# A recurrence and a dense layer in one kernel: sharing weight pieces between two leading units, loading operands once, and filler products

## The chip, the cores and the metric

The kernel runs on one core of one Trainium2 chip. The metric is device time in microseconds (us); a median of several executions is given with lowest and highest. The trace of one execution has its own length, the span, which is a few us shorter (before: 714.8 us span, 716.6 us as that execution was timed). Before the change the time is 720.13 us, median of 3 runs (718.22 to 721.48). No run below is marked as slow in the record, so all can be compared, and all gave the right result.

Engines: TensorE (PE in the profile; PEld is its loading of stationary operands), VectorE (DVE), ScalarE (ACT), GpSimd (POOL), SyncE (SP). PEclk is the clock granted to TensorE, as a share of full speed.

## The reference

```python
batch, n_heads, seq, head_dim = 4, 8, 768, 48        # d_model = 384, d_ff = 2048
for t in range(S):                                    # gated recurrence, per head
    state = alpha[:, :, t, :, None] * state + einsum('bhd,bhe->bhde', k[:, :, t], v[:, :, t])
    y[:, :, t] = einsum('bhd,bhde->bhe', q[:, :, t], state)
x = y.transpose(0, 2, 1, 3).reshape(B * S, H * D)     # 3072 tokens x 384
h = x @ w_in                                          # dense part
out = (h - tanh(h)) @ w_out
```

The weights arrive as 8-byte floats; the kernel converts them on the chip.

## The kernel before

Work is cut into 12 units of 256 tokens, three per batch. Each unit has a recurrence (`gla`), done in two chunks of 128 tokens, and a dense part (`moe`) of eight pieces: for each piece 12 matmul records (entries of the trace; a product of the program shows as two) of a first product `h`, a shrink (four instructions on ScalarE, three on VectorE), and 8 records of a second product `o`. While the dense part of one unit runs, the recurrence of the next is threaded between its pieces. The order on every engine is fixed by positions in a list:

```python
put(at, do, *args)        # one step of work at position `at`; all are sorted by `at` and issued in that order
...
moe(0, (31, 34, 37, 46, 53, 60, 68, 76), (40, 43, 50, 57, 65, 72, 79.5, 83))
STEP = 6.6
for u in range(1, NU):
    t0 = 78 + (u - 1) * FS * STEP                     # unit u's pieces follow those of unit u-1
    moe(u, [t0 + s * STEP for s in range(FS)], [t0 + (s + 2.5) * STEP for s in range(FS)])
```

At the start the weights are converted piece by piece (16 pieces): two ScalarE instructions, three VectorE instructions (source lines L65, L67, L69), one GpSimd addition. Unit 0 uses each piece as it becomes ready; unit 1 begins when unit 0 is done.

One chunk of the recurrence on TensorE, with what reads its results:

```python
def back():      tp = ps_y.tile(..., name="tp", tag="tp")       # 4 transposes of kT
def natural():   A.copy(kn, tp)                                 # ScalarE
def update():    up = ps_y.tile(..., name="up", tag="tp")       # up = kn * v, in the bank of tp
def state():     V.tensor_add(new, old, up)                     # VectorE, the state sum
def scores():    sc0, sc1 = ps_sc.tile(...), ps_sc.tile(...)    # k * q, a bank for each half of the heads
def masked():    V.tensor_mul(pm, sc, mask)
def products():  y = ps_y.tile(..., name="y", tag="y")          # from pm, v and the old state
```

TensorE's results go to PSUM. The Trainium skill, "PSUM — Partial Sum Buffer", Specifications (TRN2), gives eight banks of 512 FP32 values per partition. The program agrees: two for `h`, two for `sc0` and `sc1`, one for `y`, one that `tp` and `up` share, two for the accumulators `o0` and `o1`. All eight are taken.

## Time and profile before

| | before |
|---|---|
| time | 720.13 us (718.22 to 721.48) |
| span, granted clock | 714.8 us, 0.975 |
| TensorE / VectorE / ScalarE busy | 87% / 63% / 46% |
| first product `h` of unit 0, of unit 2 | 44.7 us, 183.0 us (the prediction has 183.1) |
| TensorE from unit 2's first product to its last | 524.2 us |

The prediction shows the slices and the waits of the first 160 us. For the rest, these are all of TensorE's waits after 180 us (columns: engine, operation, source line, what it waited for; then us in total, times, longest):

```profile
PE up L503 <- ACT kn L497: 12.5, 9, 1.6
PE sc L451 <- POOL qT L417: 9.6, 9, 1.4
PE tp L492 <- POOL kT L417: 1.7, 2, 0.8
```

So 23.8 us of 535 are lost in the steady part, nearly all of it at two places of each unit: before `up` and before `sc`.

### The profile page before, as it was taken

The page shows a single profiled execution, that of the slowest core. Times are in us where ns is not written, and L with a number is a line of the kernel's source. Part 1 is how long each engine was busy: PE and PEld are TensorE (multiplying, and loading weights), DVE is VectorE, ACT ScalarE, POOL GpSimd, SP SyncE. Part 2 cuts the span into 40 slices and gives each one's busy share as a digit, 9 for nine tenths or more (in the row PEclk, how much of TensorE's full clock was granted, in tenths as well). Part 3 has the DMA queues.
Part 4 walks back from the last instruction along what each step waited for, and adds up shares of the span by engine and source line. Part 5 has one row for each costly group of instructions (what it writes and reads, how often), then busy time and mean ns, then how long its engine had stood idle before and what let it go on. Part 6 is the DMA issues. An engine that isn't in the chain of part 4 may idle for free.

```text
span 714.8 us, 8728 instructions
## 1 busy us (share of the span) xinstructions
PE 621.6 (87%) x3089; PEld 460.4 (64%) x3089; DVE 451.3 (63%) x639; ACT 329.2 (46%) x701; POOL 115.9 (16%) x98
## 2 busy tenths in 40 slices
PE   0655586879989989989989989989989989989995
PEld 0543365657757767767767667767767767767773
DVE  4749877783683783682783773773874864874341
ACT  1435355544544544544634534634544444444451
POOL 2522543130020030030020120030110120120000
PEclk9978799999999999999999999999999999999998
DMA  9996556300801701701702602602603503500000
GB/s 181 213 178 146 107 141 164 58 1 18 160 1 28 150 1 31 146 1 37 141 1 55 122 1 54 124 1 60 118 1 81 97 1 81 98 0 7 23 0 28
DMA packets 57268, 50.99 MB, mean 71 GB/s; under 512 B 29440, under 2 KB 52096, under 8 KB 57216
## 3 DMA queue, kind: packets, MB, share of 16 engines
q1 hardware_dynamic: 54560, 49.20, 33.0%
q10 hardware_dynamic: 2656, 1.15, 1.0%
q8 instruction: 26, 0.43, 0.3%
q14 instruction: 26, 0.21, 0.1%
HBM read 44.43 MB, written 4.72 MB: 69 GB/s over the span
## 4 chain that ended last, share of the span: by engine, by line
PE 45%; DVE 27%; DMA 15%; POOL 5%; issue 3%; ACT 2%; SPq 2%; DVEq 0%; POOLq 0%; ACTq 0%
PE h L534 21%; PE o L558 15%; DVE W L411 6%; DMA qr<-in_q_dram 6%; DMA raw<-in_moe_w_in_dram 4%; DMA ar<-in_alpha_dram 3%; PE sc L451 3%; DVE kT L381 3%; DVE qT L381 3%; DVE z L546 3%; POOL qT L417 3%; DVE U L395 3%; PE y L476 3%; DVE w L545 3%; DVE aT L381 3%
## 5 line engine op out<-in xcount | busy, mean ns | idle before, releaser
L534 PE MATMUL h<-xT,w_in 128*128 128x256 f32 x1152 | 275.8, 391 | 22.9 <-POOL w_in L72 15.3
L558 PE MATMUL o<-w_out,g 128*128 128x384 f32 x768 | 267.0, 491 | 11.4 <-POOL w_out L72 11.4
L534 PEld LDWEIGHTS h<-xT,w_in 128*128 128x128 f32 x1152 | 221.7, 195 | 72.1 <-POOL w_in L72 17.6
L558 PEld LDWEIGHTS o<-w_out,g 128*128 128x128 f32 x768 | 144.3, 191 | 95.3 <-POOL w_out L72 13.1
L542 ACT ACTIVATE u<-h 128x512 f32<-128x512 f32 x96 | 57.3, 597 | 244.2 <-PE h L534 244.2
L545 DVE TENSOR_TENSOR w<-h,u 128x512 f32<-128x512 f32 x96 | 65.6, 683 | 162.6 <-ACT u L542 162.4
L417 POOL TENSOR_TENSOR kT<-kT,U 128x1024 f32<-128x1024 f32 (+1 forms) x13 | 30.3, 2331 | 377.1 <-DVE least L404 377.1
L546 DVE SCALAR_TENSOR_TENSOR z<-z,w 128x512 f32<-128x512 f32 x96 | 83.5, 869 | 10.6 <-DVE w L545 0.9
L547 DVE SCALAR_TENSOR_TENSOR g<-z,z 128x512 f32<-128x512 f32 x96 | 67.3, 701 | 10.4 <-ACT big L549 0.5
L543 ACT ACTIVATE z<-u 128x512 f32<-128x512 f32 x96 | 60.5, 630 | 3.1
L549 ACT ACTIVATE big<-u 128x512 f32<-128x512 f32 x96 | 58.9, 614 | 0.0
L544 ACT ACTIVATE z<-u 128x512 f32<-128x512 f32 x96 | 58.9, 613 | 0.0
L411 DVE TENSOR_TENSOR_SCAN W<-aT,before 128x1032 f32<-128x1032 f32 x12 | 48.7, 4059 | 0.4
L458 DVE TENSOR_TENSOR pm<-sc,mask 128x512 f32<-128x512 f32 x46 | 29.6, 685 | 16.9 <-PE sc L451 16.5
L503 PE MATMUL up<-vt,kn 128*128 128x96 f32 x160 | 22.8, 287 | 18.8 <-ACT kn L497 18.8
L417 POOL TENSOR_TENSOR qT<-qT,W 128x1024 f32<-128x1024 f32 (+1 forms) x13 | 26.7, 2053 | 65.6 <-DVE qT L381 65.6
L451 PE MATMUL sc<-qT,kT 48*128 48x128 f32 x368 | 27.6, 291 | 10.5 <-POOL qT L417 10.5
L451 PEld LDWEIGHTS sc<-qT,kT 48*128 48x128 f32 x368 | 23.1, 193 | 20.8 <-POOL qT L417 16.7
L503 PEld LDWEIGHTS up<-vt,kn 128*128 128x128 f32 x160 | 20.8, 198 | 22.6 <-ACT kn L497 22.0
L483 ACT COPY xs<-y 48x128 f32<-48x128 f32 x48 | 12.5, 260 | 46.5 <-PE y L476 46.2
L512 DVE TENSOR_TENSOR state<-state,up 48x192 f32<-48x192 f32 x32 | 11.2, 350 | 34.7 <-PE up L503 33.4
L492 PE MATMUL tp<-ident,kT 128*128 128x128 f32 x80 | 13.2, 291 | 20.1 <-POOL kT L417 20.1
(60 smaller groups left out, 444.0 us busy)
## 6 DMA issues: line engine op xcount, KB each, us to landing
raw<-in_moe_w_out_dram SPq DMA_DIRECT2D x8, 768.0 KB, 4.6
ar<-in_alpha_dram SPq DMA_DIRECT2D x24, 192.0 KB, 3.7
qr<-in_q_dram SPq DMA_DIRECT2D x24, 192.0 KB, 6.9
raw<-in_moe_w_in_dram SPq DMA_DIRECT2D x16, 288.0 KB, 7.8
out_dram<-ob SPq DMA_DIRECT2D x24, 192.0 KB, 1.9
ar<-in_alpha_dram SPq DMA_DIRECT2D x24, 176.0 KB, 4.1
qr<-in_q_dram SPq DMA_DIRECT2D x24, 176.0 KB, 6.9
kr<-in_k_dram SPq DMA_DIRECT2D x22, 192.0 KB, 5.3
```

What stands on the lines that cost most here:

```text
L381: V.transpose(t[:, g].rearrange("p c (i r) -> p r c i", r=R), raw[:, g, :, 0:32])
L411: V.tensor_tensor_scan(out=W.rearrange("p n t -> p (n t)"), data0=aT[:, 0:N * (P + 1)], data1=before, initial=0.0, op0=ALU.mult, op1=ALU.add)
L417: GP.tensor_mul(t, t, m[by].rearrange("p (g c) t -> p g c t", c=CU)[:, :, cs, 1:])
L451: T.matmul(sc[hh][:, g, :], lhsT=m["kT"][q, g, c, :], rhs=m["qT"][q, g, c, :], start=True, stop=True)
L534: T.matmul(h[:, a, :], lhsT=w_in[:, j, f * P:(f + 1) * P], rhs=xT[u][:, j, :], start=(j == 0), stop=(j == KT - 1))
L543: A.activation(z1, sq, AF.Square, bias=QB1, scale=QA)
L544: A.activation(z2, sq, AF.Square, bias=QB2, scale=QA)
L545: V.tensor_mul(w, h, sq)
L546: V.scalar_tensor_tensor(out=z1, in0=z1, scalar=QK1, in1=w, op0=ALU.add, op1=ALU.mult)
L547: V.scalar_tensor_tensor(out=g, in0=z2, scalar=QK2, in1=z1, op0=ALU.add, op1=ALU.mult)
L549: A.activation(big, sq, AF.Relu, bias=-U_MAX, accum_out=over[:, n:n + 1])
L558: T.matmul(o[c], lhsT=g[:, a * TU + c * P:a * TU + (c + 1) * P], rhs=w_out[:, f, :], start=(f == 0), stop=(f == FT - 1))
```

## The change

Its intent: the start is slow because pieces of weights trickle in and one unit does not have enough work for each. Let units 0 and 1 both use a piece as it comes. That needs four output accumulators, hence two more PSUM banks, which `y` and `tp`/`up` give up. To free the DMA queues, each operand is loaded once, and the shifted second copy is made on the chip (`widen`, six ScalarE copies per unit). Fillers keep TensorE's clock up in three waits of the first 36 us. Cut to its core:

```diff
-        ps_y = ctx.enter_context(tc.tile_pool(name="ps_y", bufs=1, space=PSUM))
...
-                    for dq in range(2):                       # load: each operand twice, shifted by 32
-                        queue.dma_start(out=t[at:at + 32]..., in_=src[:, :, 32 * dq:])
+                queue.dma_start(out=t[HP * hh:HP * hh + 32]..., in_=...)          # once
...
+            def aside(name):                                  # bank of y, and of tp and up
+                if u < 2:
+                    return ps_o.tile(..., tag="o2" if name == "y" else "o3")
+                return ps_sc.tile(..., tag="sc0" if name == "y" else "sc1")
+            def widen(what, hh):
+                to, of = t[r0 + 32:r0 + HP, :, :, 0:D - 32], t[r0:r0 + 32, :, :, 32:D]
+                A.copy(to, of)                                # one of unit 0 on VectorE
...
-                    y = m["y"] = ps_y.tile(..., name="y", tag="y")
+                    y = m["y"] = aside("y")                   # likewise tp and up
...
-                o.extend(ps_o.tile([P, d_model], FP32, name=f"o{c}") for c in range(CU))
+                o.extend(ps_o.tile([P, d_model], FP32, name=f"o{CU * (u % 2) + c}") for c in range(CU))
...
+        put(1, spin, 36); put(17, spin, 8); put(28.5, spin, 22)        # identity times identity
...
-        moe(0, (31, 34, 37, 46, 53, 60, 68, 76), (40, 43, 50, 57, 65, 72, 79.5, 83))
+        moe(0, (34, 37, 43, 50, 57, 65, 76, 87), (40, 46, 53, 59, 68, 79, 90, 97))
+        moe(1, (62, 71, 82, 93, 98.5, 104, 109.5, 115), (74, 84.5, 95.5, 101, 106.5, 112, 117.5, 123))
...
-                           scores=(18, 27), ..., back=(13, 30), update=(15.5, 33), moves=36.5)
+                           scores=(19, 29), ..., back=(13, 23), update=(15, 25.5), moves=38)
```

More of the change, by code (lines that the diff above doesn't have):

```diff
@@ L298, in fast @@
         for t, x in zip(raws, (1.0, 0.0, 0.0)):
-            V.memset(t[:, :, R - 1, :], x)
+            for hh in range(2):
+                V.memset(t[HP * hh + 32:HP * hh + HP, :, :, D - 32:32], x)
         N = NP * CU
@@ L314, in fast @@
             GP.memset(t, 0.0)
+        wake = consts.tile([P, 1], FP32, name="wake")
+        V.memset(wake, 1.0)
+        A.activation(wake, wake, AF.Square)
         raw_in, raw_out = {}, {}
@@ L349, in fast, with load @@
         vts, xT = {}, {}
-        def load(u):
+        def load(u, what, queue):
             b, i = divmod(u, UPB)
             t0 = i * TU
-            other = A if u == 0 else nc.sync
-            for n, (t, x) in enumerate(zip(raws, (alpha, k, q))):
-                queue = other if n == 1 else nc.sync
-                for hh in range(2):
-                    src = x[b].rearrange("(g two) s d -> two g (s d)", two=2)[hh][:, t0 * D:(t0 + TU) * D]
-                    src = src.rearrange("g (i n) -> i g n", i=32)
-                    for dq in range(2):
-                        at = 64 * hh + 32 * dq
-                        queue.dma_start(
-                            out=t[at:at + 32].rearrange("p g r d -> p g (r d)")[:, :, 0:R * D - 32 * dq],
-                            in_=src[:, :, 32 * dq:])
-            vt = vts[u] = three.tile([P, CU, H, D], FP32, name="vt")
-            for c in range(CU):
-                other.dma_start(out=vt[:, c], in_=v[b, :, t0 + c * P:t0 + (c + 1) * P, :].rearrange("h p d -> p h d"))
+            if what == 3:
+                vt = vts[u] = three.tile([P, CU, H, D], FP32, name="vt")
+                for c in range(CU):
+                    queue.dma_start(out=vt[:, c],
+                                    in_=v[b, :, t0 + c * P:t0 + (c + 1) * P, :].rearrange("h p d -> p h d"))
+                return
+            t, x = raws[what], (alpha, k, q)[what]
+            for hh in range(2):
+                src = x[b].rearrange("(g two) s d -> two g (s d)", two=2)[hh][:, t0 * D:(t0 + TU) * D]
+                queue.dma_start(out=t[HP * hh:HP * hh + 32].rearrange("p g r d -> p g (r d)"),
+                                in_=src.rearrange("g (i n) -> i g n", i=32))
         def gla(u, at):
@@ L376, in gla @@
             m = {}
+            def aside(name):
+                if u < 2:
+                    return ps_o.tile([P, NP, P], FP32, name=name, tag="o2" if name == "y" else "o3")
+                return ps_sc.tile([P, NP, P], FP32, name=name, tag="sc0" if name == "y" else "sc1")
             def flip(raw, make):
@@ L385, in new @@
                 return m[name]
+            def widen(what, hh):
+                t, r0 = raws[what], HP * hh
+                to, of = t[r0 + 32:r0 + HP, :, :, 0:D - 32], t[r0:r0 + 32, :, :, 32:D]
+                if u == 0 and what == 0 and hh == 1:
+                    V.tensor_copy(to, of)
+                else:
+                    A.copy(to, of)
+            for what, name in enumerate(("aT", "kT", "qT")):
+                for hh in range(2):
+                    put(at[name] - 1.5, widen, what, hh)
             put(at["aT"], flip, raws[0], lambda: tail[:, :, 0:P].rearrange("p (g c) t -> p g c t", c=CU))
@@ L468, in products @@
                 def products():
-                    y = m["y"] = ps_y.tile([P, NP, P], FP32, name="y", tag="y")
+                    y = m["y"] = aside("y")
                     if n > 0:
@@ L489, in back @@
                 def back():
-                    tp = m["tp"] = ps_y.tile([P, NP, P], FP32, name="tp", tag="tp")
+                    tp = m["tp"] = aside("tp")
                     for g in range(NP):
@@ L500, in update @@
                 def update():
-                    up = m["up"] = ps_y.tile([P, NP, 2, D], FP32, name="up", tag="tp")
+                    up = m["up"] = aside("up")[:, :, 0:2 * D].rearrange("p g (two d) -> p g two d", d=D)
                     for g in range(NP):
@@ L522, in moves @@
                         r0 = HP * hh + f0 - (H - 2 + hh) * D
-                        nc.sync.dma_start(out=xT[u][part, j, :], in_=m["xs"][r0:r0 + part.stop - part.start])
+                        (A if u < 2 else nc.sync).dma_start(out=xT[u][part, j, :], in_=m["xs"][r0:r0 + part.stop - part.start])
             put(at["moves"], moves)
@@ L570, in moe, with spin @@
             put(second_at[-1] + 2.8, store)
-        put(0, load, 0)
-        for at, what, s in ((0.1, fetch_in, 0), (0.2, fetch_in, 1), (0.3, fetch_out, 0), (0.4, fetch_in, 2)):
-            put(at, what, s)
-        put(20, load, 1)
+        def spin(n):
+            t = ps_o.tile([P, P], FP32, name="spin", tag="o0")
+            for _ in range(n):
+                T.matmul(t, lhsT=ident, rhs=ident, start=True, stop=True)
+        put(0, load, 0, 0, nc.sync)
+        put(0, load, 0, 1, A)
+        put(0.1, load, 0, 2, nc.sync)
@@ L577, in fast @@
+        put(0.1, load, 0, 3, A)
+        put(0.2, fetch_in, 0)
+        put(9, load, 1, 0, nc.sync)
+        put(9.1, fetch_in, 1)
+        put(14, load, 1, 1, nc.sync)
+        put(14, load, 1, 3, nc.sync)
+        put(17, load, 1, 2, nc.sync)
+        put(17.1, fetch_out, 0)
+        put(17.2, fetch_in, 2)
         for s in range(1, FS):
-            put(31 + 6 * s, fetch_out, s)
+            put(17 + 6 * s, fetch_out, s)
             if s + 2 < FS:
-                put(34 + 6 * s, fetch_in, s + 2)
@@ L581, in fast @@
-        gla(0, dict(aT=6, U=8, kT=10.3, ends=12.3, kTU=12.4, W=12.8, qT=15.2, qTW=17.2, sizeU=13.5, sizeW=18,
-                    scores=(19.4, 21.4), masked=(21.4, 23.4), decay=(0, 19.5), y=(23.4, 25.4), x=(25.3, 28),
-                    back=(14.5, 24.9), update=(16.2, 27.6), moves=29))
-        gla(1, dict(aT=34.5, U=38, kT=41.5, ends=43.5, kTU=45, W=46, qT=49, qTW=52, sizeU=42, sizeW=50,
-                    scores=(55.5, 62), masked=(57, 64), decay=(56, 63), y=(59, 67), x=(62, 70),
-                    back=(47, 68), update=(56, 70), moves=74))
@@ L587, in fast @@
-        for s, at in enumerate((15, 24.4, 28.7, 41, 48.7, 56, 64, 71)):
+                put(18 + 6 * s, fetch_in, s + 2)
+        put(1, spin, 36)
+        put(17, spin, 8)
+        put(28.5, spin, 22)
+        gla(0, dict(aT=5, U=7.5, kT=9.8, ends=11.8, kTU=11.9, W=12.3, qT=14.7, qTW=16.7, sizeU=10, sizeW=17,
+                    scores=(19, 21), masked=(21, 23), decay=(0, 19), y=(23, 25), x=(25, 27.5),
+                    back=(14, 24.5), update=(16, 27), moves=28))
+        gla(1, dict(aT=24, U=26, kT=28.5, ends=32.5, kTU=32.6, W=33, qT=37, qTW=39.5, sizeU=30, sizeW=38,
+                    scores=(43.5, 49.5), masked=(45.5, 51.5), decay=(40, 47), y=(48.5, 54), x=(51, 56.5),
+                    back=(37.5, 44.5), update=(39.5, 47), moves=57))
@@ L588, in fast @@
+        for s, at in enumerate((15, 20.5, 39, 45, 52, 62, 73, 84)):
             convert(at, round_in, s)
-        for s, at in enumerate((26.6, 37.5, 45, 52.5, 60, 67.5, 75, 79)):
+        for s, at in enumerate((29.5, 42, 48, 55, 65, 76, 87, 93)):
             convert(at, round_out, s)
-        moe(0, (31, 34, 37, 46, 53, 60, 68, 76), (40, 43, 50, 57, 65, 72, 79.5, 83))
+        moe(0, (34, 37, 43, 50, 57, 65, 76, 87), (40, 46, 53, 59, 68, 79, 90, 97))
+        moe(1, (62, 71, 82, 93, 98.5, 104, 109.5, 115), (74, 84.5, 95.5, 101, 106.5, 112, 117.5, 123))
@@ L593, in fast @@
         STEP = 6.6
-        for u in range(1, NU):
-            t0 = 78 + (u - 1) * FS * STEP
+        for u in range(2, NU):
+            t0 = 118 + (u - 2) * FS * STEP
             moe(u, [t0 + s * STEP for s in range(FS)], [t0 + (s + 2.5) * STEP for s in range(FS)])
-            if u > 1:
-                r = t0 - 46
-                put(r - 8, load, u)
-                rel = dict(aT=0, U=2.5, kT=5.5, ends=8, kTU=8, W=8.5, qT=11.5, qTW=14, sizeU=9, sizeW=12,
-                           scores=(18, 27), masked=(20, 29), decay=(16, 27), y=(23.5, 32), x=(26, 35),
-                           back=(13, 30), update=(15.5, 33), moves=36.5)
-                gla(u, {n: (r + x if not isinstance(x, tuple) else tuple(r + y for y in x))
-                        for n, x in rel.items()})
+            r = t0 - 46 if u > 2 else 75
+            for what in range(4):
+                put(r - 8 if u > 2 else 50, load, u, what, nc.sync)
+            rel = dict(aT=0, U=2.5, kT=5.5, ends=8, kTU=8, W=8.5, qT=11.5, qTW=14, sizeU=9, sizeW=12,
+                       scores=(19, 29), masked=(21, 31), decay=(16, 26.5), y=(24.5, 34), x=(27, 37),
+                       back=(13, 23), update=(15, 25.5), moves=38)
+            gla(u, {n: (r + x if not isinstance(x, tuple) else tuple(r + y for y in x))
+                    for n, x in rel.items()})
@@ L617, in fast @@
         V.tensor_reduce(out=fine[:, 0:1], in_=fine, axis=AX.X, op=ALU.min)
-        row = ps_y.tile([P, P], FP32, name="row", tag="tp")
+        row = ps_sc.tile([P, P], FP32, name="row", tag="sc0")
         T.transpose(row[0:1, :], fine[:, 0:1], ident)
```

## The prediction

> **What bounds the kernel now.** I read first the page's 40 slices (17.9 us each), then busy time by stretch, then TensorE's waits, then single instructions in order of time. The slices show two regimes:
>
> ```profile
> PE   0655586879989989989989989989989989989995
> DVE  4749877783683783682783773773874864874341
> PEclk9978799999999999999999999999999999999998
> DMA  9996556300801701701702602602603503500000
> ```
>
> From the ninth slice on TensorE (PE) is nearly full: that part is TensorE-bound. In the first eight it is at half, while VectorE (DVE) is the busier engine. Busy time by stretch, columns engine, us, instructions, then clock and DMA share, says it in numbers:
>
> ```profile
> 60.00:80.00 20.00, 10.55 (x27) 6.76 (x28) 17.79 (x22) 7.58 (x13) 9.54 (x4) 0.74 0.45 107
> 80.00:100.00 20.00, 13.71 (x75) 9.76 (x73) 16.93 (x23) 9.88 (x19) 8.54 (x6) 0.83 0.39 100
> 640.00:660.00 20.00, 20.00 (x120) 15.03 (x119) 6.62 (x10) 9.23 (x22) 0.00 (x0) 1.00 0.02 6
> ```
>
> VectorE has 17.8 of 20 us at 60 to 80 us, DMA only 0.45. What TensorE waits for, first 160 us (total, times, longest):
>
> ```profile
> PE tp L492 <- POOL kT L417: 18.4, 1, 18.4
> PE h L534 <- POOL w_in L72: 15.3, 5, 5.2
> PE o L558 <- POOL w_out L72: 11.4, 4, 5.6
> PE h L534 <- DMA xT<-xs: 7.7, 1, 7.7
> ```
>
> So: a first load and scan (18.4 us), one wait for small moves of features (7.7), and 26.7 us for weight pieces that ScalarE, VectorE and GpSimd are still converting from 8-byte to 4-byte floats. The rows of the conversion on VectorE:
>
> ```profile
> L69 DVE SCALAR_TENSOR_TENSOR mag<-raw,mag 128x768 int32<-128x768 int32 x16 | 17.4, 1086 | 0.6
> L67 DVE TENSOR_SCALAR mag<-mag 128x768 int32<-128x768 int32 x16 | 14.4, 903 | 0.6
> L65 DVE TENSOR_SCALAR mag<-mag 128x768 f32<-128x768 f32 x16 | 13.6, 851 | 1.7 <-ACT mag L61 1.6
> ```
>
> One piece costs VectorE 1.09+0.90+0.85=2.84 us; there are 16. After 160 us the waits are small and regular: 12.5 us in 9 times (up for ScalarE's copy) and 9.6 us in 9 times (sc for GpSimd's scaling of qT), about 2.5 us per unit of 52.8 us. One such place in order of time, PE's then VectorE's rows:
>
> ```profile
> 309.81 1.13 PE L503 MATMUL up<-vt,kn 128*128 128x96 f32 x8 [1.60 <-ACT kn L497]
> 310.78 2.77 PE L558 MATMUL o<-w_out,g 128*128 128x384 f32 x8
> 314.54 1.16 PE L451 MATMUL sc<-qT,kT 48*128 48x128 f32 x16 [0.98 <-POOL qT L417]
> ```
> ```profile
> 312.86 2.17 DVE L546 SCALAR_TENSOR_TENSOR z<-z,w 128x512 f32<-128x512 f32 x1
> 315.14 0.81 DVE L547 SCALAR_TENSOR_TENSOR g<-z,z 128x512 f32<-128x512 f32 x1
> 315.87 0.84 DVE L512 TENSOR_TENSOR state<-state,up 48x192 f32<-48x192 f32 x2
> ```
>
> Here sc starts at 314.54; the state sum, which reads up, ends at 316.71. Before, nobody cares. It matters below.
>
> **What the Trainium skill says.** "TensorE: Matmul & The Clock Gate", What's actually happening: the array runs at half clock until it has been busy for some 3.4 us. The trace agrees: 6 products h (12 records) take 5.0 us at 87 us, 2.6 in the steady part; the granted clock is 0.52 at 40 to 50 us. "GPSIMD Engine Reference", Specifications: GpSimd shares its SBUF interfaces with VectorE. Agrees: z above takes 2.17 us while GpSimd scales qT, 0.69 otherwise. "DMA: Bandwidth & Descriptors", Issuing engines are not separate DMA queues: another issuing engine saves only issue time. Here the issue is what hurts: the six xT moves occupy SyncE from 37.8 to 44.6 us. "Perfetto Trace Analysis", Optimization Strategy: a gap that repeats on the engine that should be full can mean too little PSUM. Before has no such gap beyond the 2.5 us; I expect the change to make one.
>
> **Part 1: the first product earlier.** alpha, k and q were loaded twice (192 and 176 KB per half), now once, with six copies of a quarter tile (about 0.55 us each, ScalarE). alpha and k of unit 0 before first use: 1.5 MB before, 0.79 now; at the 168 GB/s of the first 10 us that is 9 and 4.7 us. So the first transposes move from 10.75 to about 7.0. GpSimd also scales both halves of qT before it turns to a weight (1.8 us saved), features are ready at about 31 instead of 37.3, and their moves are issued by ScalarE (6 x 0.5 us, then 1.9 to land) and not behind SyncE's bulk loads: first h at about 36 instead of 44.7. The fillers (36, 8 and 22 products, about 0.13 us each by sc, whose 8 products or 16 records take 1.1) lie in waits of TensorE; they only keep its clock up. Removed DMA, 0.6 MB per unit, is hidden later on.
>
> **Part 2: two units per piece.** From the built order of instructions, VectorE has between the mask of unit 0's second chunk (about 27) and the fourth shrink of unit 1: 14 conversions, 39.8 us; 12 shrinks of 0.68+0.87+0.70=2.25, 27.0; recurrence of unit 1 (three transposes of 2.04 for four rows together, scans 2.31 and 4.06, two state sums 1.4, two pairs of masks 2.6, ends 0.5) 17.0; of unit 2 without masks and with one state sum 13.7. Together 97.5. From 50.8 to 134.3 us VectorE was before idle for 12.1 us between its rows, so 85% busy, with one unit to feed on; two should fill its gaps to some 94% (my choice): 97.5/0.94=104, so the fourth shrink ends at 131. Until then VectorE bounds, so doubling TensorE's work there is free. After it TensorE still has, before unit 2's first product: a mask to wait for (1.3), y (1.9), seven groups of h or second products (2.6 each, 18.2), sc and y of the next chunk (3.0): 24.4. Unit 2 starts at 155.5, and in before at 183.1. Before had then two second products of unit 1 left, after has one: 2.6 more. **Gain 27.6+2.6=30.2 us**, part 1 included.
>
> **Part 3: PSUM.** Four output accumulators (o0 to o3) take the two banks that y and tp/up had; from unit 2 on y shares the bank of sc0, tp and up that of sc1. In the built program sc1's first product waits for VectorE, that is for the state sum that reads up; the sum stands after a shrink. With the rows above: sc could start at 314.5 and now starts at 316.7, the same in every unit (2.17, 1.93 where the state is copied). The stretch of VectorE before it is unbroken from 293 to 318, so it does not move up by itself. Nine units (3 to 11) x 2.05=**18.5 us lost**. The other new dependencies (second tp after the mask, second sc after the feature copies) have one h and one second product between, and cost nothing by the same timing.
>
> **Sum.** 714.8-30.2+18.5=703.1 span; the median stands 5.3 above the profiled span (720.13 to 714.8): 708.4. Tail unchanged.
>
> **Rivals.** (a) No PSUM loss, because VectorE gets ahead: then 690. For: TensorE waits more and VectorE has slack later; against: VectorE's unbroken stretch, which starts from TensorE's own product. (b) The start stays bound by conversion with VectorE no fuller than 85%: fourth shrink at 142, so 720. For: ScalarE is in order, and now has widening copies, six DMA issues and conversions in one line; against: an out-conversion stands between each in-conversion and its shrink. (c) Raw weight pieces (four buffers) arrive late with unit 2's loads between them: SyncE is in order and waits for a buffer; some 3 to 6 us, 712 to 714. (d) The longer gap before sc drops the clock: gaps of 0.98 and 2.1 with one product between; the 3.1 us gap at 79 us did not (2.85 for 8 records after it). If it does, about 2 us more in nine units: 727.
>
> **Range and chances.** The start may err by 8 us either way, the loss by 5 down or 3 up, giving 698 to 720. Faster by 2% means under 705.7, only 2.8 below my figure; that someone tuned the positions by hand speaks for a gain. Faster 0.40, same 0.57, slower 0.03.
>
> **What would show it.** First h near 36 us; VectorE above 90% at 50 to 130; unit 2's first h near 155; waits of sc for the state sum, nine times or so, 18 us in sum. Wrong if sc's waits stay at 10 us, or if unit 2 starts after 165.

## The result

The changed kernel takes **746.25 us** (743.42 to 746.99, 4 runs) beside 719.76 us for the kernel before (718.22 to 721.48, 4 runs): ratio 1.036, 95% interval 1.0323 to 1.0397. It is slower, and outside the predicted range. All outputs are right. A ratio is always the mean time of one kernel's fast runs over that of the other's fast runs of the same rounds, so not quite the ratio of the medians quoted. The profiled span is 743.9 us, with a clock of 0.956.

The 40 slices after (18.6 us each):

```profile
PE   7758856799799799899889889989979989979996
DVE  8996758734944933953933854763773773773432
PEclk9988988899899999999989999999999999999998
```

Two things are to be seen against the rows of before. In the start TensorE is hardly fuller: 5, 8, 8, 5, 6, 7 in slices three to eight (the sevens before them are partly fillers). And in the steady part, where before had two nines and an eight in turn, the eight is often a seven now, or there are two of them; PEclk has an eight in slices eleven and 21, where before had only nines.

VectorE was to be above 90% busy from 50 to 130 us. It is not. The first row is the kernel before, the second the changed one (columns: stretch, its length, busy us of PE, PEld, DVE, ACT, POOL with their instructions, then clock, DMA share, GB/s):

```profile
50.00:130.00 80.00, 55.58 (x251) 40.29 (x250) 64.85 (x82) 42.74 (x77) 29.41 (x17) 0.87 0.63 140
50.00:130.00 80.00, 56.05 (x244) 39.23 (x244) 57.83 (x79) 44.23 (x80) 23.92 (x14) 0.87 0.49 110
```

57.83 of 80 us is 72%, and before it was 81%: with two units to feed, VectorE got less done in this stretch, not more. TensorE's waits in the first 160 us, those of weight pieces:

```profile
PE h L553 <- POOL w_in L72: 21.1, 6, 7.2
PE o L577 <- POOL w_out L72: 8.0, 5, 3.9
```

These were 15.3 and 11.4 before: 26.7, and now 29.1. The waits that sharing was to fill are still there. How VectorE comes to stand still meanwhile is seen in order of time, TensorE's rows and VectorE's:

```profile
96.77 5.32 PE L577 MATMUL o<-w_out,g 128*128 128x384 f32 x8 [3.86 <-POOL w_out L72]
101.92 2.75 PE L553 MATMUL h<-xT,w_in 128*128 128x256 f32 x12
```

```profile
97.37 0.69 DVE L566 SCALAR_TENSOR_TENSOR g<-z,z 128x512 f32<-128x512 f32 x1
105.34 0.69 DVE L564 TENSOR_TENSOR w<-h,u 128x512 f32<-128x512 f32 x1 [7.28 <-ACT u L561]
```

TensorE waits for a piece, then does `o` at half clock (5.32 us for 8 records instead of 2.6), and only then the `h` whose shrink VectorE waits for: 7.28 us idle. Nothing in that `h` needed the late piece; it stands behind `o` in a fixed order.

TensorE's waits after 180 us, to be laid beside the three lines of before:

```profile
PE up L522 <- ACT kn L516: 19.3, 9, 3.2
PE sc L470 <- DVE state L531: 9.7, 6, 1.8
PE sc L470 <- POOL qT L436: 5.9, 6, 1.0
PE tp L511 <- POOL kT L436: 5.1, 3, 1.7
PE sc L470 <- DVE state L529: 3.2, 2, 1.6
```

Together 43.2 us instead of 23.8. The waits for the state sum are new; the one for `kn` has grown. One unit in order of time, the same place that the prediction shows of before (there `up` at 309.81, `o` at 310.78, `sc` at 314.54 without a break):

```profile
310.02 0.60 PE L511 MATMUL tp<-ident,kT 128*128 128x128 f32 x4
313.14 1.81 PE L522 MATMUL up<-vt,kn 128*128 128x96 f32 x8 [2.52 <-ACT kn L516]
314.74 3.80 PE L577 MATMUL o<-w_out,g 128*128 128x384 f32 x8
318.48 0.49 PE L470 MATMUL sc<-qT,kT 48*128 48x128 f32 x2
320.19 1.13 PE L470 MATMUL sc<-qT,kT 48*128 48x128 f32 x14 [1.22 <-DVE state L531]
321.24 2.86 PE L553 MATMUL h<-xT,w_in 128*128 128x256 f32 x12
```

and VectorE's row that releases it, which reads `up` and so frees the bank of `sc1`:

```profile
319.20 0.84 DVE L531 TENSOR_TENSOR state<-state,up 48x192 f32<-48x192 f32 x2
```

Now `sc` starts, stops after its first two records (one product each in `sc0` and `sc1`; the second part waits), and goes on when the state sum is done. Besides, `up` and `o` take 1.81 and 3.80 us instead of 1.13 and 2.77: half clock.

**Where the 29.1 us of span came from** (743.9 against 714.8). Unit 2's first product comes at 177.6 instead of 183.0, with 2.6 us less of unit 1 left to do: 8.0 us gained, where 30.2 were predicted. From there on 37.1 us are lost, where 18.5 were predicted (37.1 less 8.0 is the difference of 29.1).

### The profile page after: what moved, and what is told of

Same layout as the page of the kernel before. It is cut to its first block, busy times and chain, and to the rows that moved or that the text cites. A ratio compares the mean times of both kernels' runs of the same rounds, so it can differ in the third digit from the quotient of the medians.

```text
span 743.9 us, 8951 instructions
## 1 busy us (share of the span) xinstructions
PE 653.7 (88%) x3221; PEld 486.7 (65%) x3221; DVE 452.0 (61%) x644; ACT 373.6 (50%) x773; POOL 118.6 (16%) x98
## 4 chain that ended last, share of the span: by engine, by line
PE 56%; DVE 25%; ACT 6%; POOL 5%; issue 4%; DMA 3%; ACTq 1%; DVEq 0%; SPq 0%; POOLq 0%
PE h L553 24%; PE o L577 21%; DVE W L430 6%; PE sc L470 3%; PE y L495 3%; DVE U L414 3%; DVE kT L390 3%; DVE z L565 3%; DVE aT L390 2%; DVE qT L390 2%; PE y L491 2%; DVE w L564 2%; POOL qT L436 2%; ACT ar L402 1%; POOL state L482 1%
## 5 line engine op out<-in xcount | busy, mean ns | idle before, releaser
L553 PE MATMUL h<-xT,w_in 128*128 128x256 f32 x1152 | 279.1, 395 | 23.7 <-POOL w_in L72 21.1
L577 PE MATMUL o<-w_out,g 128*128 128x384 f32 x768 | 272.8, 501 | 8.0 <-POOL w_out L72 8.0
L553 PEld LDWEIGHTS h<-xT,w_in 128*128 128x128 f32 x1152 | 225.5, 198 | 74.6 <-POOL w_in L72 23.8
L577 PEld LDWEIGHTS o<-w_out,g 128*128 128x128 f32 x768 | 146.6, 195 | 96.2 <-POOL w_out L72 9.9
L470 PE MATMUL sc<-qT,kT 48*128 48x128 f32 x368 | 32.4, 297 | 18.9 <-DVE state L531 9.7
L470 PEld LDWEIGHTS sc<-qT,kT 48*128 48x128 f32 x368 | 26.4, 196 | 30.3 <-issue 20.6
L522 PE MATMUL up<-vt,kn 128*128 128x96 f32 x160 | 24.4, 300 | 20.7 <-ACT kn L516 20.7
L390 DVE STREAM_TRANSPOSE aT<-ar 128x256 f32<-128x256 f32 x48 | 24.5, 625 | 7.3 <-ACT ar L402 7.1
L482 POOL TENSOR_TENSOR state<-state,ends 48x192 f32<-48x192 f32 x40 | 27.1, 677 | 7.0 <-DVE state L529 5.0
L414 DVE TENSOR_TENSOR_SCAN U<-aT,after 128x1032 f32<-128x1032 f32 x12 | 27.7, 2307 | 0.5
```

Of the source, the lines that this page charges most:

```text
L390: V.transpose(t[:, g].rearrange("p c (i r) -> p r c i", r=R), raw[:, g, :, 0:32])
L470: T.matmul(sc[hh][:, g, :], lhsT=m["kT"][q, g, c, :], rhs=m["qT"][q, g, c, :], start=True, stop=True)
L553: T.matmul(h[:, a, :], lhsT=w_in[:, j, f * P:(f + 1) * P], rhs=xT[u][:, j, :], start=(j == 0), stop=(j == KT - 1))
L577: T.matmul(o[c], lhsT=g[:, a * TU + c * P:a * TU + (c + 1) * P], rhs=w_out[:, f, :], start=(f == 0), stop=(f == FT - 1))
```

## The experiments

Theory after the result: the steady loss has three parts, the shared bank, the widening copies on ScalarE, and the clock that falls behind longer gaps; the start lost its gain to waits of a fixed order. Rivals are named in the expectations. To read the results, one measure of the steady part is used throughout. It is taken from TensorE's rows in order of time, in the seven of nine units where nothing stands between `tp` and `up`: the distance from the start of `tp` to that of `up`, and from `up` to the first product after `sc`. Medians, in us:

| kernel | tp to up | up to after sc | TensorE, unit 2's first product to its last | of it idle | half-clock groups, excess |
|---|---|---|---|---|---|
| before | 2.22 | 5.82 | 524.2 (521.6 with the 2.6 taken off) | 23.7 | 0 |
| after | 3.11 | 8.10 | 559.4 | 43.3 | 13.2 |
| a_twice | 2.23 | 8.11 | 558.5 | 38.4 | 18.3 |
| a_own | 3.11 | 6.45 | 538.6 | 28.5 | 11.7 |
| a_both | 2.23 | 5.82 | 526.1 | 24.8 | 3.0 |
| b_bank | 2.22 | 8.10 | 561.1 | 39.2 | 17.9 |
| b_widen | 3.11 | 5.82 | 533.4 | 28.1 | 4.3 |
| c_spin | 3.11 | 8.09 | 551.4 | 14.8 (and 38.2 in fillers) | 0 |

A group's excess is the time to the next group's start, less idle time, less its usual time per record; groups over 0.5 us are added up. The last column depends on what is taken as usual: with the median of each kind it is up to 2 us higher. The variants of the changed kernel have one `o` of unit 1 left when unit 2 starts and are to be compared with 521.6; b_bank and b_widen have two, as before, and are to be compared with 524.2.

### Four runs on the parts: a_twice, a_own, a_both, b_bank

Beside 720.06 us of the kernel before.

**a_twice**: the changed kernel, but from unit 2 on loaded twice again and without widening.

```diff
+                for dq in range(2 if u >= 2 else 1):
...
-                for hh in range(2):
+                for hh in range(2 if u < 2 else 0):
                     put(at[name] - 1.5, widen, what, hh)
```

> The changed kernel, but from unit 2 on alpha, k and q are loaded twice again as in before, so ScalarE makes no widening copies there; the shared banks stay. My theory: in the steady part the copies put 0.9 us before the first transpose of each unit, which lengthens the wait of up for kn from 1.6 to 2.5 us; without them the wait returns to 1.6 in each unit, 8 us of idle go, and the slow o products behind that wait (three units, about 1.7 us each) go with it: about 733, sum of TensorE's waits after unit 2 near 35 us instead of 43. Rival A (all of the steady loss is the shared bank and the clock drop behind its wait): 744 or more, as sc's wait only grows by what kn's loses. Rival B (the granted clock drops for a reason unrelated to the gaps): the slow groups stay, about 738.

Measured: 743.41 us (742.63 to 745.94), ratio 1.0335 (1.029 to 1.038). The copies gone, `tp` to `up` is back at 2.23, and yet only some 3 us are gained, not the expected 13. The table tells why: idle time fell by 4.9 us, but the half-clock groups grew by 5.1.

**a_own**: the changed kernel with banks of their own for `y` and `tp`/`up` from unit 3 on (unit 2 still shares, because its recurrence runs while unit 1 holds o2 and o3); copies kept.

```diff
-                if u < 2:
+                if u != 2:
                     return ps_o.tile(...)
...
-                o.extend(... name=f"o{CU * (u % 2) + c}" ...)
+                o.extend(... name=f"o{CU * (u == 1) + c}" ...)
```

> The changed kernel, but only unit 1 uses accumulators o2 and o3, and from unit 3 on y and tp/up use those two banks, so sc no longer waits for the state sum; the widening copies stay. My theory: the waits of sc for the state sum vanish (12.9 us), those for qT come back to about 1 us per unit, and the slow h behind sc (four units, some 1.9 us each) vanish: about 746 less 11 less 8, so 727; kn waits stay at 2.5 us. Rival A (all of the steady loss is the bank): 712. Rival B (clock unrelated to gaps): 735.

Measured: 723.57 us (721.8 to 726.17), ratio 1.0047 (0.9998 to 1.0095). By medians of different rounds some 23 us come from the bank alone. No wait for the state sum is left.

**a_both**: both edits.

> Both edits: no widening from unit 2 on and banks of their own. My theory: the steady part is that of before again (per unit 1.6 us for kn, 1.0 for qT, no slow groups); what is left is the start, 8 us better than before by the time at which unit 2 begins, so 711 against 720 of before. Rival (the sum of the two is not all, the steady part has lost something else): 716 or more. Rival B (clock unrelated to gaps): mean granted clock stays at 0.956 and 725.

Measured: 710.27 us (709.35 to 711.89), ratio 0.9871 (0.9831 to 0.991), as expected. With the bank and the copies undone from unit 2 on, what is left of the change gains 1.3%, and the steady part is before's again (2.23 and 5.82).

**b_bank**: the other way round: the kernel before, with the shared bank and the changed positions of the recurrence from unit 3 on, nothing else. (The positions do not confuse the test: a_both has them too, with banks of their own, and its steady part is that of before.)

```diff
+            def aside(name):
+                if u < 3:
+                    return ps_y.tile(..., tag="y" if name == "y" else "tp")
+                return ps_sc.tile(..., tag="sc0" if name == "y" else "sc1")
...
+                if u > 2:
+                    rel.update(scores=(19, 29), ..., back=(13, 23), update=(15, 25.5), moves=38)
```

> The kernel before, with one part of the change alone: from unit 3 on y shares sc0's bank and tp/up sc1's, with the positions that the change gives to the recurrence. My theory: sc waits 2 us more in each of nine units, 18.5 us as predicted, and some slow groups behind it, so 740 to 748. Rival (the wait is harmless without the widening copies, as kn's gap is 1.6 and the clock holds): 738, exactly the 18.5 us. Rival A (the bank costs nothing by itself): 720.

Measured: 750.75 us (748.56 to 757.65), ratio 1.0439 (1.0364 to 1.0514). The shared bank costs the kernel before some 31 us, more than the whole change costs. TensorE's rows at one such place:

```profile
381.07 1.98 PE L456 MATMUL sc<-qT,kT 48*128 48x128 f32 x14 [1.60 <-DVE state L515]
382.99 5.30 PE L539 MATMUL h<-xT,w_in 128*128 128x256 f32 x12
```

The wait of 1.60 us (after one of 0.99 before the first part of `sc`) is followed by `h` at half clock, 5.30 us instead of 2.6. Such a group stands in eight units. So the effects of bank and copies do not add: the copies cost 13.3 us with own banks (a_own less a_both) and 3 with the shared bank.

### What holds the steady part: c_fill, a_ownfill, b_widen, a_fill

**a_fill** (beside 717.47): a_both, with work put into the two waits: a second product between `tp` and `up`, a first product before `sc`.

```diff
-                scores=(19, 29), ... update=(15, 25.5)
+                scores=(19.7, 29), ... update=(16.4, 25.5)
```

> a_both with two positions moved in units 2 on: up stands after the next second product instead of directly after tp, and sc after the next h instead of before it. My theory: TensorE then has a group of 2.6 us to do while ScalarE copies kn and GpSimd scales qT, so the 1.6 and 1.0 us of waiting per unit (24 us after 180 us in a_both) go almost wholly: 688 to 690. Rival (the recurrence chain itself sets the pace and the wait only moves to the masks and y): 700 to 710.

Measured: 687.25 us (686.68 to 687.51), ratio 0.957 (0.9524 to 0.9615), as expected. TensorE's waits after 180 us:

```profile
PE sc L473 <- POOL qT L439: 3.1, 7, 1.0
PE tp L514 <- POOL kT L439: 2.4, 3, 0.8
PE up L525 <- ACT kn L519: 0.6, 1, 0.6
```

23.8 us of waits have become 6.1, and no half-clock group is left. These waits were in the kernel before too: two positions in the list are worth more than the whole change was meant to bring. (No run moved them in the kernel before by itself.)

**c_fill** (beside 720.14, as the next two): the same two positions in the changed kernel, bank and copies as they are.

> The changed kernel with shared banks and widening copies left in, and only the two positions of a_fill moved (up after the next second product, sc after the next h). My theory: kn's wait is hidden, but sc still waits for the state sum, which itself comes later because up does; some 3 us of waiting per unit are left and the clock still drops behind them: 730 to 738. Rival (moving TensorE's order hides all of it): 692.

Measured: 727.09 us (725.0 to 730.13), ratio 1.0111 (1.0064 to 1.0157); 3 us below the expected range. The wait for `kn` has all but gone (0.6 us), and with it go most of the 19 us gained beside the changed kernel (different rounds). That for the state sum stays (14.4 us): moving `sc` does not help where the bank ties it to VectorE. The clock record still shows seven drops in the steady part.

**a_ownfill**: a_fill with the copies kept.

> a_fill with the single load and the widening copies kept in all units (banks of their own, the two moved positions). My theory: the 0.9 us that the copies put into the chain is covered by the second product of 2.6 us: 687 to 691. Rival (the copies cost their 13 us wherever the waits are): 698 to 701.

Measured: 694.85 us (694.08 to 696.84), ratio 0.9662 (0.9627 to 0.9697), between both expectations. The copies cost 7.6 us beside a_fill, by medians of different rounds, even though the wait for `kn` is filled. The waits for qT and kT (6.8 and 5.1 us, instead of 3.1 and 2.4) account for 6.4 of it. That widened operands are ready later is the likely reason; it was not looked at further.

**b_widen**: the kernel before with single loads and copies from unit 2 on.

> The kernel before, with one part of the change alone: from unit 2 on a single load and widening copies by ScalarE. My theory (a_own against a_both: 13 us for the copies): kn's wait grows from 1.6 to 2.5 us in nine or ten units and in some of them the clock drops: 728 to 734. Rival (the copies are hidden, and cost only with the shared bank): 720.

Measured: 730.5 us (727.99 to 736.08), ratio 1.0174 (1.0122 to 1.0226), as expected. Loading once instead of twice saves traffic that nothing waited for and puts copies where something does.

### The clock apart from the waits: c_spin

No run so far changes the clock alone: each edit moved the waits too. **c_spin** (beside 720.68) is the changed kernel with fillers in the waits of units 3 to 11; it shortens no wait.

```diff
+            if u > 2:
+                put(r + 14.99, spin, 10, f"o{CU * (u % 2)}")     # before up
+                put(r + 18.99, spin, 8, f"o{CU * (u % 2)}")      # before the first sc
```

> The changed kernel, with products of the identity into an output accumulator that is free at the time, in units 3 to 11: ten before the product up (the wait for kn, 2.1 us on average) and eight before the first scores (the wait for the state sum, 1.6 us), about 0.13 us each at full clock, so 1.3 and 1.0 us, which lie inside the waits. They shorten no wait for data. Theory clock (about half of the loss is half-clock groups behind the gaps): the slow groups of o and h (4 to 5 us instead of 2.6) go, the waits for data stay, mean clock from 0.956 to 0.97 or more, and the time falls from 746 to 729 to 735. Rival (the waits are the whole loss, and slow groups are a side effect of the profile or have another cause): 746, or up to 10 us more where fillers overrun a wait, slow groups in 7 units as before.

Measured: 739.62 us (739.16 to 740.35), ratio 1.0279 (1.0226 to 1.0332), clock 0.981, no slow group. It gained 6.6 us, not 11 to 17. The same place as above:

```profile
308.42 0.60 PE L511 MATMUL tp<-ident,kT 128*128 128x128 f32 x4
308.86 2.40 PE L595 MATMUL spin<-ident 128*128 128x128 f32 x20
311.53 1.13 PE L522 MATMUL up<-vt,kn 128*128 128x96 f32 x8 [0.27 <-ACT kn L516]
...
315.10 1.95 PE L595 MATMUL spin<-ident 128*128 128x128 f32 x16
...
318.57 1.13 PE L470 MATMUL sc<-qT,kT 48*128 48x128 f32 x14 [1.10 <-DVE state L531]
319.63 2.86 PE L553 MATMUL h<-xT,w_in 128*128 128x256 f32 x12
```

A filler product is two records, so it takes twice what I had reckoned, but it delays nothing here: `tp` to `up` is 3.11 us as in the changed kernel (3.12), and `up` to `h` 8.10 in both, although there `up` and `o` ran at half clock. That is the point: a slow `o` lies inside the wait for the state sum and costs nothing; only a slow `h` behind `sc` comes on top. In the changed kernel four units have a slow `h` (6.8 us of the excess) and three a slow `o`. So my share of one half was wrong: of 37.8 us that TensorE loses after unit 2's start (0.7 more than the span loses, which has a shorter tail), 559.4 less 551.4, so about 8, are the clock, and 29.8 remain as waits for data at full clock. They can be added up: 9 x 2.28 for `up` to after `sc` is 20.5, 7 x 0.89 for `tp` to `up` is 6.2, and the wait of `tp` grew by 3.5 to 5.1: together 30.2. Of the 8 us, 6.3 reach the span of c_spin, because its tail after the last product is 8.6 us instead of 7.0; why is not known.

It probably explains a_twice too. In the changed kernel the clock fell at `up` or `o` in three units, and in these `h` was not slow. Without copies, it falls at `sc` in most units, and `h` pays (eight units). That both belong together is read off the traces; it was not tested by itself.

When the clock falls can be read from the traces' clock records, which the experiments above did not use. In each of the 16 runs all drops to half clock begin on one grid with steps of 3.413 us, and in the steady part they last one step or two. I cut each run after 190 us into these steps, left out those already at half clock, and took TensorE's busy share of each. All 26 steps under 45% busy were followed by a drop, 20 of 54 between 45 and 56%, and 1 of 2216 above that. So it is not one gap that counts but what falls into one step: in the changed kernel the step from 309.99 to 313.40, with the `tp` and the wait for `kn`, was 26% busy, and the clock fell at 313.40. In the kernel before no step after 190 us was under 52%. Earlier in the runs the picture is less sharp: the step with the prediction's gap of 3.1 us at 79 us was 43% busy, and no drop followed. And the same wait can be cut by the grid in one unit and not in another, which is a likely reason why only some units show a drop. (The ends of matmuls are modelled, so the shares are approximate.)

### The start: a_nospin, b_early, a_sc, best, best2

**a_nospin** (beside 717.47, as the next two): a_both without the 66 fillers of the first 36 us.

> a_both without the 66 filler products. My theory: the fillers lie in waits and only warm the clock; the first two h after 37 us then run at half clock and some recurrence products too, costing 2 to 4 us at the first h, but VectorE is what is late at that point, so 710 to 713 by the end. Rival C (the fillers are what the 8 us gain of the start come from): 716 or more. Rival D (they hold up the in-order TensorE): below 709.

Measured: 710.3 us (709.75 to 712.8), ratio 0.9899 (0.9848 to 0.995). The fillers are worth nothing that can be measured.

**b_early**: a_both without sharing: the earlier start, then before's positions and two accumulators.

> a_both with nothing shared: unit 1 runs after unit 0 by the positions of before, while the early start (single load with copies for units 0 and 1, moves issued by ScalarE, fillers) stays. My theory, from the times at which unit 2 begins (183.1 in before, 177.6 in after, with one group of 2.6 us less to follow): if sharing fills VectorE no better than before, all of the 8 us come from the first h being 7.5 us earlier, and this kernel gives 710 to 713 as well. Rival F (sharing gives the gain, the earlier start is lost again): 718 to 720.

Measured: 715.8 us (713.1 to 716.68), ratio 0.9958 (0.9905 to 1.001), not the expected 710 to 713. Unit 2 begins at 183.2 us, as before. What a_both gains at the start (unit 2 at 174.7) thus hangs on sharing. It is no clean test of the earlier first product: that came at 39.2 us here, but TensorE waited three times (8.4 us) for moves of features, so most of it only ran from 45.9.

**a_sc**: a_both with unit 1's first `sc` ahead of the third `h` (scores at 42.9 instead of 43.5), against a wait of VectorE near 57 us (5.0 us in the changed kernel, 3.7 in a_both).

> a_both with unit 1's first scores put ahead of the third h of unit 0 in TensorE's order. My theory: the start is late because engines that run in a fixed order wait for one another: VectorE sits idle 5 us near 57 us for a mask whose scores stand behind an h that waits for a converted piece. With the scores ahead that idle goes, unit 2 starts 3 to 5 us earlier: 705 to 707. Rival E (the sheer work of conversion, or the arrival of the pieces by DMA, sets the pace): unchanged, 710.

Measured: 708.8 us (707.56 to 709.59), ratio 0.9872 (0.9825 to 0.992). About 1.5 us by medians against a_both, not 3 to 5; the ratios do not tell them apart.

**best** (beside 720.14): a_fill with that position and two more of the start.

```diff
-                    scores=(43.5, 49.5), ...
+                    scores=(42.9, 49.5), ...
-        for s, at in enumerate((15, 20.5, 39, 45, 52, 62, 73, 84)):
+        for s, at in enumerate((15, 20.5, 39, 45, 52, 62, 73, 81.5)):
-        moe(1, (62, 71, 82, ...
+        moe(1, (62, 67.5, 82, ...
```

> a_fill with three positions of the start moved: unit 1's first scores ahead of unit 0's third h, unit 1's second h directly after unit 0's sixth (ahead of a second product that waits for a converted w_out piece), and the last w_in piece converted before the long scan of unit 2. My theory (fixed orders make the engines of the start wait for one another, VectorE is not full): VectorE's idle of 7 us near 100 us and TensorE's wait of 7 us near 130 us go, unit 2 starts 6 to 10 us earlier than in a_fill (176.0): 677 to 681. Rival E (the work of conversion sets the pace): unit 2 starts within 2 us of a_fill's, 685 to 687.

Measured: 682.09 us (681.08 to 682.82), ratio 0.9479 (0.9446 to 0.9512); 1 us above the expected range. Unit 2 begins at 170.8 instead of 176.0. But one wait has grown, that before the seventh `o` of unit 0 (1.0 us in a_fill). TensorE's row in best:

```profile
130.24 4.64 PE L580 MATMUL o<-w_out,g 128*128 128x384 f32 x8 [9.12 <-POOL w_out L72]
```

From 107.7 to 131.6 us VectorE has no gap there, and the conversion of this piece stands behind its scan of 3.8 us. A conversion step here (128x768 integers) also took 2.41 us at 112.4 us, while GpSimd scaled kT from 112.05 to 114.40, and 0.56 us at 137.2, without.

**best2** (beside 720.68): best with that one conversion ahead of the scan.

```diff
-        for s, at in enumerate((29.5, 42, 48, 55, 65, 76, 87, 93)):
+        for s, at in enumerate((29.5, 42, 48, 55, 65, 76, 80.9, 93)):
             convert(at, round_out, s)
```

> As best, with the out-conversion of piece 6 moved from 87 to 80.9 in the list, so that VectorE does it before the long scan of unit 2 and not after it. Theory order (the wait of 9.1 us before the seventh second product of unit 0 is only VectorE's order): that wait falls to 3 us or less, unit 2's first product comes 3 to 5 us before 170.8, time 677 to 679. Rival amount (VectorE has no gap from 108 to 131 us, so the scan, the state sum and the next conversion come later by as much and the wait turns up elsewhere): unit 2 within 1.5 us of 170.8, time 681 to 683.

Measured: **676.11 us** (674.9 to 676.6), ratio 0.9391 (0.9342 to 0.944). That is 0.9 us below the expected range. Unit 2 begins at 165.6, 5 us earlier. The wait was a matter of order, although another has come in its place, shorter but before a product at half clock. TensorE's row in best2:

```profile
121.23 5.45 PE L556 MATMUL h<-xT,w_in 128*128 128x256 f32 x12 [5.01 <-POOL w_in L72]
```

This version is 6% faster than the kernel before and 9% faster than the changed one (676.11 against 746.25, of different rounds).

## Why the prediction was wrong

Its span was 703.1; 743.9 was measured. The 40.8 us between them are 22.1 in the start (unit 2 at 177.6 instead of 155.5; after 165 was the prediction's own sign of being wrong) and 18.7 in the steady part (37.1 instead of 18.5, and 0.1 from taking 183.1 for 183.0).

**Part 1, the first product earlier: right, and worth little.** Predicted at about 36 us, measured 37.2. Then TensorE waits for pieces all the same: its third `h` comes at 54.7 after 6.3 us of waiting, where before it ran from 52.9. The fillers do nothing (a_nospin).

**Part 2: the step that failed is "two should fill its gaps to some 94% (my choice)".** The work was counted nearly right: VectorE is busy for 94.2 us between 27 and 149 us, where the prediction had 97.5. The fourth shrink of unit 1 ends at 149.05 and not at 131, so the fill is 97.5/122, 80% by the prediction's count and 77% by the measured one, even less than the 85% of rival (b). (That 85% left out short pauses between rows; the trace has 68.7 of 83.5 us busy, 82%.) The tail from there was counted as 24.4 us and is 28.5. What stands in place of the failed step: in this fixed order the two units did not fill each other's gaps, since each engine waits for the first thing in its list and the other unit's work stands behind it. The order as a cause is shown, in part: moving four positions in the start takes unit 2 from 176.0 (a_fill) to 165.6, and best2 alone, by one position, 5 us. In best2 the fourth shrink ends at 137.6, a fill of 97.5/110.6, 88%. Whether 94% can be reached by order at all, and where the remaining 10 us to 155.5 go, stays open. Two rivals can be read off the traces. Late raw pieces (c): ScalarE's first step of a conversion waits for one once, 2.6 us at 21 us in the changed kernel, and never after that; in best2 it is likewise the second piece alone (4.5 us at 23). ScalarE late with its steps of the conversion (b): from 25 to 150 us VectorE waits 0.9 us for these in the changed kernel, but 15.7 us for `u`, for whose `h` ScalarE in turn waits 26.0 us on TensorE, and 5.0 us for scores.

**Part 3, the shared bank: the mechanism was right, its size nearly so.** Predicted 2.05 us in nine units, 18.5; the distance grew by 2.28, in nine units 20.5. As waits of `sc` for the state sum only 12.9 us show, eight times, because a slow `o` eats part of the wait and the first two records of `sc` run before it. What was missing in the sum were two other terms:

- **Copies on ScalarE**, which appear in the prediction only for the start (part 1 and rival (b)). They delay `kn` and kT: 6.2 us and most of the 3.5 us more before `tp`. b_widen, with 10.4 us on the kernel before, shows them alone. A gap of TensorE that waits for ScalarE in every unit (12.5 us, nine times) was quoted in the prediction; work added to that engine had to be asked about there.
- **The clock, rival (d).** It was put aside because one gap of 3.1 us at 79 us had not lowered the clock. It happened: about 8 us in the changed kernel (c_spin). The rival's sum, 2 us in each of nine units, was twice that, since the clock fell in seven of them, and where the slow group is `o`, it is hidden.

Rival (a) did not happen. The removed DMA, 51.0 to 38.0 MB in all, was hidden as predicted: a_twice brings the second loads of ten units back and loses nothing. (It is 1.1 MB per unit, not the 0.6 of the prediction: three operands, two halves, 176 KB each.) The 5.3 us between median and span were 2.4 this time.

## What to carry to other kernels

Count a stage's work, but do not set its fill by choice: in a fixed order, look for each engine at what stands first in its list when a shared resource is late, and at what is stuck behind it. A PSUM bank given up was a new dependency here, in every repetition, on the reader of what now shares it; and work added to a spare engine costs if the bound engine waits for that engine anywhere. Before restructuring, fill the waits that repeat: two positions in the list gained some 22 us (a_both to a_fill, by their ratios 0.9871 and 0.957) where the whole change lost 26. For the clock, look at how busy TensorE is over stretches of some 3.4 us (the grid above), not only at the longest gap.

## What the Trainium skill lacked or had wrong

- "TensorE: Matmul & The Clock Gate", What's actually happening, says the array falls to half clock after an idle window of about 3.4 us. In these runs no single gap in the steady part was so long, and still groups ran at half clock: `h` took 5.30 us after gaps of 0.99 and 1.60 us with one 0.48 us part of `sc` between them (b_bank), and `up` and `o` ran slow after 0.60 us of `tp` and a single gap of 2.52 us (after). Gaps of 1.60 and 0.98 us with an `o` of 2.77 us between them (before) never did it, and the same gap lowered the clock in some units and not in others. The window need not be idle: after 190 us all 26 steps of 3.413 us with TensorE under 45% busy were followed by a drop, and 1 of 2216 above 56%. The same page, A second HAM failure mode: psum-queue depth-cycling, names frequent short idles as a cause, but gives no length; these are lengths.
- The same page, Loop structure matters more than you think, proposes keeping the array busy by the order of loops. No point of it says what filler products do in a wait on data: 36 records of about 0.118 us in each of nine units raised the mean clock from 0.956 to 0.981 and gained 6.6 us (c_spin); 66 products in the first 36 us gained nothing (a_nospin).
